# Weight words called for earlier, and the first feed-forward block in the third step, in a fused mLSTM and multiplicative FFN kernel

## The chip, the cores and the metric

The kernel runs on one core of a Trainium2 chip. The metric is device time of one execution in microseconds (us); the figure for the kernel before is the median of seven runs. A profile shows one execution: TensorE (PE, with weight loads as PEld), VectorE (DVE), ScalarE (ACT), GpSimd (POOL), and the queue of SyncE (SP), which issues most of the DMAs.

## The reference, cut to what matters

```python
batch, n_heads, seq, head_dim = (4, 8, 768, 40)      # q, k, v, gates
n_tokens, d_model, d_ff = (3072, 320, 1024)          # w1, w2, w3, w_out (float64 arrays)
for t in range(S):                                   # mLSTM cell
    m_new = max(f[t] + m, i[t])
    C = exp(f[t] + m - m_new) * C + exp(i[t] - m_new) * outer(v[t], k[t])
    n = exp(f[t] + m - m_new) * n + exp(i[t] - m_new) * k[t]
    y[t] = sigmoid(o[t]) * (C @ q[t]) / max(abs(n . q[t]), 1)
x = y as rows of (batch, seq), columns (head, dim)   # 3072 x 320
out = (((x @ w1) * (x @ w2)) @ w3) @ w_out
```

## The kernel before, in words

**The cell** is computed in chunks. A unit n = (c, b) is 128 tokens (the chunk pair c) of one batch b, all 8 heads; there are 24 units, numbered with the batch running fastest. The main loop (L733) makes steps s = 0 to 31. In step s, `quarter_work` (L328) computes on PE the scores `ss` and the new state terms `pc` of unit s, and, for unit s-1, the products `ph` (weights times v) and `pi` (state times q); DVE then makes the output y of unit s-1 (`outputs`, L397: `h`, `den`, y). PE works on quarters of 64 rows and 64 columns, four side by side. For the first `N_DIAG` units (5) `ph` is instead made with heads on the diagonal quarters only, in a bank of its own, and one DVE addition of 328 columns (L405) takes the place of four of 164 (L408).

**What a unit needs.** k and q of the unit are turned (`turn`, L301: eight PE transposes into `pt`, two ACT copies to `kT` and `qT`; from unit 10 by DVE). Its weights `pw` are exp of a row vector of U, spread over 128 partitions, plus a bias (`weights`, L288: eight ACT instructions), masked by POOL (`masks`). U's rows come in one of three ways: by `spread` (L263), sixteen PE matmuls into `ub`, for units 0 to 3; by `rows_of_u` (L283), a DVE transpose of `UT`, for units 4 to 9; and by a DMA from a copy in DRAM, `U_d`, from unit 10. `cols_of_u` (L273) makes `UT` on PE (`pu`) and ACT, at the end of step 1. `weighted` (L317, POOL) scales v.

**The feed-forward part.** `up` and `up_rest` (L588, L601) make one block: for 256 tokens (half of a group of four units) and 256 of the 1024 columns, a = x w1 and b = x w2, each as 8 matmuls of 128 by 256 for the first 256 rows of w and then a rest on quarters for the last 64 rows (`wr`), followed by an ACT copy of a and a DVE product `ab`. x comes from y by `x_trans` (L456): POOL doubles 64 columns (`twice`, L453), three PE transposes `px`, one ACT copy `xT`. 24 blocks are made so, `n_up` (L722) to a step: one in steps 4 and 5, two in steps 6 to 16. Group 0's blocks run over columns 0 to 511 of both halves first. Later groups go by another scheme (`up_by_seven`), which the change leaves alone. w3 and w_out are multiplied into `w3o` in the steps 10 to 17 (`fold`, L244, PE `wp`), and `ffn_out` makes the result.

**Weights come as float64.** `fetch` (L202) has SP load a piece as pairs of 32-bit words (512 KB for w1 and w2) into one of four `raw` buffers, or, first, into `idle` memory (two places in w3o). `scale` (L178) scales the two words, the high one on ACT and the low one on ACT or, with `early`, on DVE; `to_f32` (L188) joins them with two DVE instructions. w1 and w2 are ten pieces in two halves of the columns: for each half four of 128 rows and `wr`. After them come eight of w_out (`wo`) and sixteen of w3. `n_cvt` gives the pieces converted at the end of a step, `n_fetch` the pieces called for by then.

**What sets the order.** PE's instructions are issued in the order of the program (`in_order`, L84), those of ACT, DVE, POOL and SP as well (`keep_order`, L524). So an instruction that waits holds up all behind it on its engine: on SP, a load that waits for a free buffer holds up the loads after it. Four PSUM banks (`mps`, L77) are handed out in turn to `pt`, `px`, `ub`, `ph`, `pa`, `pb` and `wp`. In step s SP calls for unit s+2 (L737).

Of the kernel before, what the change touches and what calls it, by code (L numbers as in the profile page):

```python
# [16 lines left out]
def kernel(  # L17
# [83 lines left out]

    NB, NBQ, NBV = 4, 3, 5
    N_DVE = N_U = 10
    N_DIAG = 5
    q_all = const.tile([P, NBQ * H * DP], FP, name="q_all")
    qbuf = [q_all[:, i * H * DP:(i + 1) * H * DP].rearrange("p (h d) -> p h d", d=DP) for i in range(NBQ)]
    kbuf = [const.tile([P, H, DP], FP, name=f"kbuf{i}") for i in range(NB)]
# [4 lines left out]
    gT = const.tile([P, NT2, BH], FP, name="gT")  # L112
    wT = const.tile([P, NT2, BH], FP, name="wT")
    decay = const.tile([P, B * NP, NT], FP, name="decay")
    UT = const.tile([P, 2, 2, BH], FP, name="UT")
    U_d = dram.tile([NT, BH, L], FP, name="U_d")
    NY = 15
    KC = KF + 1
# [152 lines left out]
        return ub  # L271

    def cols_of_u():  # L273
        pu = mps([P, 2, 2, BH], "pu")
        for x in range(2):
            for e in range(2):
                for t in range(2):
                    for i in range(2):
                        t0 = (1 - i) * P + x * L + t * 32
                        mm(pu[x * L + e * 32:x * L + (e + 1) * 32, t, i], U[:, t0:t0 + 32], ident[0:RG, i * BH:(i + 1) * BH])  # L280
        nc.scalar.copy(out=UT, in_=pu)

    def rows_of_u(n):  # L283
        c, b = divmod(n, B)
        nc.vector.transpose(out=weights_tile(n).rearrange("p h (t i) -> p h t i", t=2),
                            in_=UT[:, :, c - 1, b * H:(b + 1) * H].rearrange("p t h -> p h t").unsqueeze(3).to_broadcast([P, H, 2, 32]))

    def weights(n):  # L288
        c, b = divmod(n, B)
        src = weights_tile(n) if c else spread(n)  # L290
        pw = weights_tile(n)
        for h in range(H):
            nc.scalar.activation(out=pw[:, h, :], in_=src[:, h, :], func=AF.Exp, bias=aT[:, c, b * H + h:b * H + h + 1])  # L293
# [31 lines left out]
        nc.gpsimd.tensor_tensor(out=new, in0=old, op=OP.mult, in1=decay[:, b * NP:(b + 1) * NP, 2 * c + x:2 * c + x + 1]  # L325
                                .to_broadcast([P, NP, D1]))

    def quarter_work(s, rest):  # L328


        rest()

        def part(j, c0, n):
            return cell[j][:, :, c0:c0 + NP * n].rearrange("p x (n d) -> p x n d", d=n)

        ss, pc, pi = part(0, 0, L), part(0, NP * L, D1), part(1, 0, D1)
        ph = [cell[1][:, x, NP * D1:2 * NP * D1].rearrange("p (h d) -> p h d", d=D1) for x in range(2)]
        n = s - 1
        if 0 <= n < NU:
            pw, vt, qT = u_t.pop(n), vbuf[n % NBV], qT_t.pop(n)  # L340
            before = before_t.pop(n)

            if n < N_DIAG:
                ph = mps([P, H, D1], "ph")
                for hq in range(H):
                    for r in halves:
                        mm(ph[r, hq, :], pw[r, hq, :], vt[r, hq, :])
            for hd in range(H // 2 if n >= N_DIAG else 0):
                for x, e in quarters:
                    hq = hd if x == e else hd + H // 2  # L350
                    mm(ph[x][halves[e], hd, :], pw[halves[x], hq, :], vt[halves[x], hq, :])
            for p in range(NP):
                for hip, x in quarters:
                    mm(pi[halves[x], hip, p, :], qT[heads[hip], p, halves[x]], before[x][heads[hip], p, :])
        n, first_read = s, None
        if n < NU:
            c, b = divmod(n, B)
            kt, vw = kbuf[n % NB], vw_t.pop(n)
            ends = range(2 if c < NT2 - 1 else 1)
            first, second, after = state[b]  # L360
            before_t[n] = first, second
            state[b] = after, second, first
            kT, qT, pw = kT_t.pop(n), qT_t[n], u_t[n]
            for p in range(NP):
                for hip, x in quarters:
                    mm(ss[halves[x], hip, p, :], kT[heads[hip], p, halves[x]], qT[heads[hip], p, halves[x]])
            for p in range(NP):
                for x, e in quarters:
                    if x in ends:
                        mm(pc[halves[e], x, p, :], kt[halves[x], 2 * p + e, :], vw[halves[x], 2 * p + e, :])  # L370
        den = None
        if 0 <= s - 1 < NU:
            den = outputs(s - 1, pi, ph)
            den()
        if n < NU:
            pv = pw.rearrange("p (n two) t -> p two n t", two=2)
            first_read = nc.vector.tensor_tensor(out=pv, in0=ss, in1=pv, op=OP.mult)
        with tc.issue_after(first_read.ins) if first_read else nullcontext():
            if den:
                den()  # L380
            if n < NU:

                if c:
                    nc.vector.tensor_tensor(out=second, in0=pc[:, 0], in1=second, op=OP.add)  # L384
                else:
                    nc.vector.tensor_copy(out=second, in_=pc[:, 0])
                if len(ends) > 1:
                    decayed(after, second, n, 1)
            if den:
                den()  # L390
            if n < NU and len(ends) > 1:
                nc.vector.tensor_tensor(out=after, in0=pc[:, 1], in1=after, op=OP.add)
            if den:
                done = den()
        return done if den else first_read
# [89 lines left out]
        nc.sync.dma_start(out=f_sb[r], in_=f_gate.rearrange("b h s -> (b h) s")[:, cs])  # L485
        nc.scalar.dma_start(out=a[r], in_=i_gate.rearrange("b h s -> (b h) s")[:, cs])

    w3o_words = w3o.rearrange("p f d -> p (f d)").bitcast(U32).rearrange("p (n two) -> p n two", two=2)
    load(0, slice(0, 2))
    fetch("w12", 0, 0)  # L490
    load(0, slice(2, 3))
    fetch("w12", 1, 0)
    load(1, slice(0, 2))
    load_o(0)
    load(1, slice(2, 3))
    load_o(1)
    fetch("w12", 2, 0)
    idle += [w3o_words[:, i * CW:(i + 1) * CW] for i in range(2)]

    nc.vector.memset(on, 1.0)  # L500
    nc.vector.memset(on.rearrange("p (c t) -> p c t", t=L)[:, :, 0:1], 0.0)
# [73 lines left out]
    pd = mps([P, B * NP * NT], "pd")  # L575
    for x in range(2):
        mm(pd[halves[x]], odd[:, x].to_broadcast([RG, L]), pick.rearrange("p j g c -> p (j g c)"))
    nc.scalar.copy(out=decay.rearrange("p j c -> p (j c)"), in_=pd)
    nc.scalar.activation(out=g, in_=U, func=AF.Exp)
    scale_next(True)  # L580
    convert()
# [121 lines left out]
    def ffn_out(blocks, pos=None):  # L703
# [5 lines left out]
        for (gr, j), po in zip(blocks, pos):  # L709
# [3 lines left out]
            nc.scalar.dma_start(out=out[t0:t0 + P, :], in_=o_sb)  # L713


    ups = [(0, [f, f + 1], slice(j * 2 * P, (j + 1) * 2 * P)) for part in range(0, FO, FO // 2) for j in range(2)
           for f in range(part, part + FO // 2, 2)]
    ups += [(gr, [f, f + 1], slice(j * 2 * P, (j + 1) * 2 * P)) for gr in range(1, 3) for j in range(2)
            for f in range(0, FO, 2)]
    downs = [(gr, j) for gr in range(NG) for j in range(GT)]  # L720
    sevens = [(gr, f) for gr in range(3, NG) for f in range(FH)]
    n_up = [0] * 4 + [1] * 2 + [2] * 11 + [0] * 15  # L722
    n_seven = [0] * 19 + [1] * 12 + [0]
    n_down = [0] * 17 + [2] * 6 + [1] * 7 + [0, 5]
    w12 = [("w12", i, part) for part in range(2) for i in range(2 * KF + 1)]
    todo = w12[3:] + [("wo", i, 0) for i in range(FO)] + [("w3", ko, part) for ko in range(FO) for part in range(2)]
    n_cvt = [0, 1, 1, 1, 2, 2, 3, 4, 4] + [2] * 7
    n_fetch = [4, 5, 7, 9, 11, 13, 16, 20]
    pinned, ahead = 32, 9
    behind = ExitStack()  # L730
    turned, converted, fetched = 0, 2, 3

    for s in range(len(n_up)):  # L733
        if N_U <= s + 3 < NU:
            load_u(s + 3)
        if s + 2 < NU:
            load(s + 2)  # L737
            load_o(s + 2)
        if s < NU:
# [1 line left out]
                decayed(state[s % B][1], state[s % B][0], s, 0)  # L741
        if NY <= s - 2 < NU:
            send(s - 2)
        elif 0 <= s - 2 < NY:
            twice(s - 2)
        if NY <= s - 2 < NU:
            get_back(s - 2)
# [16 lines left out]
        if seven and s > NU:  # L764
            seven[0]()
        now = [ups.pop(0) for _ in range(n_up[s])]
        open_ups = [up(*x) for x in now]
        def rest():
            for x in open_ups:
                up_rest(*x)  # L770
            if seven:
                seven[2]()

        gated = None
        if s <= NU:
            gated = quarter_work(s, rest)
        else:
            rest()
        with tc.issue_after(gated.ins) if gated else nullcontext():
            if seven:  # L780
                seven[3]()
            if NY <= s - 2 < NU:
                x_turn(s - 2)
            for n in (B, B + 1) if s == 2 else (s + 3,):
                if 2 <= s and n < N_U:
                    rows_of_u(n)
            if N_DVE <= s + 1 < NU:
                gated = turn(s + 1)
# [2 lines left out]
            if s - 2 in range(4 * GT - 1, NU, GT):  # L791
                token_sums((s - 2) // GT)
        if s == 0:
            gate_cols(g, gT, nc.scalar.copy)
        if s == NU:
            cell_psum.close()
            banks.extend([ps_m] * 3 + [ctx.enter_context(tc.tile_pool(name="ps_x", bufs=4, space=bass.MemoryType.PSUM))] * 4)
        if s + 1 < N_DVE:
            turn(s + 1)
            while turned < min(s - 1, NY):  # L800
                x_trans(turned)
                turned += 1
        if s < NU:
            if s + 1 < NU:
                weighted(s + 1)
                weights(s + 1)
                masks(s + 1)
            out_gate(s)
        if s == 1:
            cols_of_u()  # L810
        if s == 0:
            for i, r in enumerate(third):
                nc.sync.dma_start(out=U_d[i * GC:(i + 1) * GC].rearrange("c r t -> r c t"), in_=U3[r])
        with tc.issue_after(gated.ins) if N_DVE <= s + 1 < NU else nullcontext():
            for _ in range(n_cvt[s] if s < len(n_cvt) else 0):
                convert()
                converted += 1
        if s >= ahead:
# [40 lines left out]
```

## Time and profile before

| what | value |
|---|---|
| median of 7 runs | 443.18 us (440.09 to 447.0) |
| time of the profiled execution | 444.08 us |
| its span, first to last instruction | 442.4 us |
| PE busy | 424.6 us, 96% |
| DVE, ACT, POOL busy | 305.4, 150.7, 82.5 us |
| moved by DMA | 51.14 MB, mean 116 GB/s |
| PE waiting for `xT` (ACT L464), for k's DMA, for `wr` (DVE L191) | 4.0, 5.7, 1.2 us |

Busy time is the time in which an engine has an instruction under way. A matmul's duration overlaps its neighbours', so the spacing of groups, as the chain of waits shows it, says more of PE's pace than the mean of one. In a row of the timeline the columns are start and duration of a run of like instructions, engine, line, operation, what is written and read, shape, count, and in brackets how long the engine had been idle before and what released it.

### The profile page before, as it was taken

What the parts mean: (1) busy time and instruction counts of PE and PEld (TensorE: products, weight loads), DVE (VectorE), ACT (ScalarE), POOL (GpSimd) and SP (SyncE); (2) the same over time, 40 slices, a digit from 0 to 9 for tenths busy, and PEclk for the clock granted to TensorE, in tenths of its full rate; (3) what the DMA queues carried; (4) which work ended last, traced back from release to release, by engine and by line L of the source; (5) the groups of instructions that cost most, each with busy time, mean ns of one, the idle gap of its engine ahead of it and who ended that gap; (6) DMA issues with size and microseconds to landing.
All of it is one profiled execution on the core that took longest, in us unless ns stands there. A gap on an engine that the chain in (4) does not pass through costs nothing.

```text
span 442.4 us, 12852 instructions
## 1 busy us (share of the span) xinstructions
PE 424.6 (96%) x5303; PEld 338.0 (76%) x5303; DVE 305.4 (69%) x629; ACT 150.7 (34%) x409; POOL 82.5 (19%) x155
## 2 busy tenths in 40 slices
PE   4997989999799999999999999999999999999996
PEld 3886878877678787887867877868778777777774
DVE  6358668769777797797758769759689776444800
ACT  4557656756454255233303320313210111101110
POOL 3425333321230331133022204202000000000000
PEclk9999999999899999999999999999999999999999
DMA  8999695787997667778456376454121110000001
GB/s 186 172 186 198 142 178 89 168 208 197 191 199 184 167 132 173 184 147 145 96 107 142 88 144 141 116 103 99 46 51 29 39 39 16 15 16 16 1 30 45
DMA packets 135211, 51.14 MB, mean 116 GB/s; under 512 B 109360, under 2 KB 126960, under 8 KB 135152
## 3 DMA queue, kind: packets, MB, share of 16 engines
q1 hardware_dynamic: 131552, 46.29, 51.1%
q10 hardware_dynamic: 3600, 4.03, 2.6%
q8 instruction: 41, 0.67, 0.7%
q14 instruction: 18, 0.15, 0.1%
HBM read 44.50 MB, written 5.80 MB: 114 GB/s over the span
## 4 chain that ended last, share of the span: by engine, by line
PE 91%; DMA 3%; issue 2%; DVE 1%; ACT 1%; SPq 1%; POOL 0%; ACTq 0%; DVEq 0%
PE cell L92 24%; PE pa L92 22%; PE po L92 14%; PE pb L92 14%; PE wp L92 7%; PE p L92 5%; PE pt L95 3%; DMA kbuf<-in_k_dram 2%; PE ub L92 1%; PE px L95 1%; PE ph L92 1%; DMA raw<-in_moe_w_dram 1%; ACT pw L293 0%; DVE h L408 0%; DVE ab L609 0%
## 5 line engine op out<-in xcount | busy, mean ns | idle before, releaser
L92 PE MATMUL pa<-xT,w 128*128 128x256 f32 x240 | 61.6, 388 | 4.0 <-ACT xT L464 4.0
L92 PE MATMUL po<-w3o,ab 128*128 128x320 f32 x224 | 61.8, 433 | 0.0
L92 PEld LDWEIGHTS po<-w3o,ab 128*128 128x128 f32 x224 | 42.5, 190 | 17.2 <-issue 0.4
L92 PEld LDWEIGHTS pa<-xT,w 128*128 128x128 f32 x240 | 45.1, 192 | 12.1 <-ACT xT L464 4.9
L325 POOL TENSOR_TENSOR state<-state,decay 128x164 f32<-128x164 f32 x40 | 19.7, 492 | 174.3 <-DVE state L384 151.1
L298 POOL TENSOR_SCALAR_AFFINE_SELECT pw<-pw 64x512 f32<-64x512 f32 x48 | 37.2, 775 | 56.7 <-ACT pw L293 55.1
L92 PE MATMUL pb<-xT,w 128*128 128x256 f32 x192 | 46.1, 384 | 0.0
L92 PE MATMUL cell<-w3o,ab 128*128 128x320 f32 x160 | 44.0, 432 | 0.0
L293 ACT ACTIVATE pw<-pw,aT 128x64 f32<-128x64 f32 x160 | 40.3, 339 | 2.8 <-ACT o_sb L711 2.8
L92 PEld LDWEIGHTS pb<-xT,w 128*128 128x128 f32 x192 | 37.1, 194 | 5.3
L92 PEld LDWEIGHTS cell<-w3o,ab 128*128 128x128 f32 x160 | 30.5, 190 | 12.0
L92 PE MATMUL pa<-xT,wr 64*64 64x256 f32 x384 | 36.8, 386 | 1.2 <-DVE wr L191 1.2
L656 DVE SCALAR_TENSOR_TENSOR a_sb<-pa,wo 128x512 f32<-128x512 f32 x12 | 8.3, 692 | 41.6 <-PE pa L92 41.6
L608 ACT ACTIVATE a_sb<-pa 128x512 f32<-128x512 f32 x24 | 14.3, 596 | 66.1 <-PE pb L92 66.1
L92 PE MATMUL pb<-xT,wr 64*64 64x256 f32 x384 | 36.2, 380 | 0.0
L92 PE MATMUL wp<-wo,w3T 128*128 128x320 f32 x128 | 35.9, 433 | 0.0
L609 DVE TENSOR_TENSOR ab<-pb,a_sb 128x512 f32<-128x512 f32 x24 | 16.4, 689 | 27.8 <-ACT a_sb L608 27.8
L92 PEld LDWEIGHTS pa<-xT,wr 64*64 64x64 f32 x384 | 19.0, 132 | 16.1 <-issue 8.3
L92 PEld LDWEIGHTS wp<-wo,w3T 128*128 128x128 f32 x128 | 23.7, 190 | 8.9
L711 ACT COPY o_sb<-po 128x320 f32<-128x320 f32 x14 | 6.0, 425 | 67.4 <-PE po L92 67.4
L408 DVE TENSOR_TENSOR h<-cell,h 64x164 f32<-64x164 f32 x76 | 24.7, 326 | 1.4
L92 PEld LDWEIGHTS pb<-xT,wr 64*64 64x64 f32 x384 | 20.2, 133 | 3.0
(135 smaller groups left out, 738.3 us busy)
## 6 DMA issues: line engine op xcount, KB each, us to landing
raw<-in_moe_w_dram SPq DMA_DIRECT2D x64, 128.0 KB, 3.2
kbuf<-in_k_dram SPq DMA_DIRECT2D x24, 160.0 KB, 4.7
vbuf<-in_v_dram SPq DMA_DIRECT2D x24, 160.0 KB, 4.9
o_in<-in_o_gate_dram SPq DMA_DIRECT2D x24, 160.0 KB, 4.6
out_dram<-o_sb ACTq DMA_DIRECT2D x24, 160.0 KB, 1.8
raw<-in_moe_w_dram SPq DMA_DIRECT2D x7, 512.0 KB, 4.9
pw<-U_d SPq DMA_DIRECT2D x28, 128.0 KB, 3.3
raw<-in_moe_w_out_dram SPq DMA_DIRECT2D x8, 320.0 KB, 3.5
```

The costliest lines, as they stand in the source:

```text
L92: in_order(nc.tensor.matmul(out, lhsT=lhsT, rhs=rhs, start=start, stop=stop))
L95: in_order(nc.tensor.transpose(out, in_, ident[0:n, 0:n]))
L293: nc.scalar.activation(out=pw[:, h, :], in_=src[:, h, :], func=AF.Exp, bias=aT[:, c, b * H + h:b * H + h + 1])
L298: nc.gpsimd.affine_select(out=pw[r], in_=pw[r], compare_op=OP.is_ge, fill=0.0, base=0, pattern=[[0, H], [1, L]], channel_multiplier=-1)
L325: nc.gpsimd.tensor_tensor(out=new, in0=old, op=OP.mult, in1=decay[:, b * NP:(b + 1) * NP, 2 * c + x:2 * c + x + 1] .to_broadcast([P, NP, D1]))
L408: nc.vector.tensor_tensor(out=part, in0=ph[x][halves[e]], in1=part, op=OP.add)
L608: nc.scalar.mul(out=a_sb, in_=pa, mul=UP ** -2)
L609: nc.vector.tensor_tensor(out=ab_t[gr][j][:, fs[0]:fs[-1] + 1, t0:t0 + a_sb.shape[-1]], in0=pb, in1=a_sb, op=OP.mult)
L656: nc.vector.scalar_tensor_tensor(out=out, in0=p, scalar=UP ** -2, in1=q, op0=OP.mult, op1=OP.add)
L711: nc.scalar.copy(out=o_sb, in_=po)
```

## The change

- **Words.** Before the loop, five pieces of w1 and w2 are called for in place of three (the whole first half of the columns); the output gate of unit 0 goes behind the third piece and that of unit 1 behind the fourth, and two places in `wo` are added to the idle memory. In step 2 SP is given the other five, three ahead of the k and q of unit 4 and two ahead of its v. Conversions are moved accordingly (`n_cvt`, `between`, `rest`).
- **Blocks.** Group 0's blocks take all 1024 columns of its first 256 tokens first. `n_up` becomes one in steps 2 to 5, two in 6 to 14, one in 15 and 16. The block of step 2 is made in the middle of `quarter_work`, by `between`, after the outputs of unit 1 are complete and before the scores of unit 2. `turn(2)` and `turn(3)` move to steps 2 and 3.
- **U's rows.** `cols_of_u` moves ahead of the loop and gets a third chunk; `rows_of_u` also serves units 1 to 3. The write of `U_d` moves from step 0 to step 4.
- **Units 2 to 4** make `ph` on quarters (`N_DIAG` is 2).

```diff
-    N_DIAG = 5
+    N_DIAG = 2
...
     def weights(n):
         c, b = divmod(n, B)
-        src = weights_tile(n) if c else spread(n)
+        src = weights_tile(n) if n else spread(n)
...
+        den = None
+        if 0 <= s - 1 < NU:
+            den = outputs(s - 1, pi, ph)
+            den()
+            if between:
+                for _ in range(3):
+                    den()
+                den = None
+                between()
         n, first_read = s, None
...
     load(0, slice(0, 2))
     fetch("w12", 0, 0)
     load(0, slice(2, 3))
     fetch("w12", 1, 0)
-    load(1, slice(0, 2))
+    load(1)
+    fetch("w12", 2, 0)
     load_o(0)
-    load(1, slice(2, 3))
+    idle += [words[:, i * CW:(i + 1) * CW] for words in (w3o_words, wo_words) for i in range(2)]
+    fetch("w12", 3, 0)
     load_o(1)
-    fetch("w12", 2, 0)
-    idle += [w3o_words[:, i * CW:(i + 1) * CW] for i in range(2)]
+    fetch("w12", 4, 0)
...
+    cols_of_u()
     nc.scalar.copy(out=decay.rearrange("p j c -> p (j c)"), in_=pd)
+    rows_of_u(1)
...
-    n_up = [0] * 4 + [1] * 2 + [2] * 11 + [0] * 15
+    n_up = [0] * 2 + [1] * 4 + [2] * 9 + [1] * 2 + [0] * 15
...
-    n_cvt = [0, 1, 1, 1, 2, 2, 3, 4, 4] + [2] * 7
-    n_fetch = [4, 5, 7, 9, 11, 13, 16, 20]
+    n_cvt = [1, 0, 3, 0, 1, 2, 2, 3, 2] + [2] * 7
+    n_fetch = [5, 5, 10]
...
-        if s + 2 < NU:
+        if s < 3:
+            if s == 2:
+                for _ in range(3):
+                    fetch(*todo.pop(0))
+            load(s + 2, slice(0, 2))
+            if s == 1:
+                load_o(2)
+            if s == 2:
+                for _ in range(2):
+                    fetch(*todo.pop(0))
+                fetched = 10
+            load(s + 2, slice(2, 3))
+            if s:
+                load_o(s + 2)
+        elif s + 2 < NU:
...
+        if s == 3:
+            turn(3)
         def rest():
             for x in open_ups:
                 up_rest(*x)
             if seven:
                 seven[2]()
+            if s == 3:
+                for _ in range(2):
+                    convert()
+
+        def between():
+            twice(1)
+            weighted(2)
+            for n in range(2):
+                x_trans(n)
+            for _ in range(2):
+                scale_next(True)
+                convert()
+            turn(2)
+            for x in now:
+                up_rest(*up(*x))
...
-            for n in (B, B + 1) if s == 2 else (s + 3,):
-                if 2 <= s and n < N_U:
+            for n in (s + 2,) if s < B else (s + 2, s + 3) if s == B else (s + 3,):
+                if n < N_U:
                     rows_of_u(n)
```

More of the change, by code (lines that the diff above doesn't have):

```diff
@@ L114 @@
     decay = const.tile([P, B * NP, NT], FP, name="decay")
-    UT = const.tile([P, 2, 2, BH], FP, name="UT")
+    UT = const.tile([P, 2, 3, BH], FP, name="UT")
     U_d = dram.tile([NT, BH, L], FP, name="U_d")
@@ L273, in cols_of_u @@
     def cols_of_u():
-        pu = mps([P, 2, 2, BH], "pu")
+        pu = mps([P, 2, 3, BH], "pu")
         for x in range(2):
@@ L277, in cols_of_u @@
                 for t in range(2):
-                    for i in range(2):
-                        t0 = (1 - i) * P + x * L + t * 32
-                        mm(pu[x * L + e * 32:x * L + (e + 1) * 32, t, i], U[:, t0:t0 + 32], ident[0:RG, i * BH:(i + 1) * BH])
+                    for c, of in ((0, slice(0, 2)), (1, slice(2, 3))):
+                        t0 = c * P + x * L + t * 32
+                        mm(pu[x * L + e * 32:x * L + (e + 1) * 32, t, of].rearrange("p c r -> p (c r)"),
+                           U[:, t0:t0 + 32], ident[0:RG, 0:(of.stop - of.start) * BH])
         nc.scalar.copy(out=UT, in_=pu)
@@ L285, in rows_of_u @@
         nc.vector.transpose(out=weights_tile(n).rearrange("p h (t i) -> p h t i", t=2),
[L286 removed]
+                            in_=UT[:, :, (0, 2, 1)[c], b * H:(b + 1) * H].rearrange("p t h -> p h t").unsqueeze(3).to_broadcast([P, H, 2, 32]))
     def weights(n):
         c, b = divmod(n, B)
[L290 removed]
+        src = weights_tile(n) if n else spread(n)
         pw = weights_tile(n)
@@ L326, in decayed, with quarter_work @@
                                 .to_broadcast([P, NP, D1]))
-    def quarter_work(s, rest):
+    def quarter_work(s, rest, between):
         rest()
@@ L370, in quarter_work @@
                         mm(pc[halves[e], x, p, :], kt[halves[x], 2 * p + e, :], vw[halves[x], 2 * p + e, :])
[L371 to L374, printed above, removed]
         if n < NU:
@@ L486 @@
         nc.scalar.dma_start(out=a[r], in_=i_gate.rearrange("b h s -> (b h) s")[:, cs])
-    w3o_words = w3o.rearrange("p f d -> p (f d)").bitcast(U32).rearrange("p (n two) -> p n two", two=2)
+    w3o_words, wo_words = (t.rearrange("p f d -> p (f d)").bitcast(U32).rearrange("p (n two) -> p n two", two=2)
+                           for t in (w3o, wo))
     load(0, slice(0, 2))
@@ L713, in ffn_out @@
             nc.scalar.dma_start(out=out[t0:t0 + P, :], in_=o_sb)
[L716 to L719, printed above, removed]
+    ups = [(gr, [f, f + 1], slice(j * 2 * P, (j + 1) * 2 * P)) for gr in range(3) for j in range(2)
+           for f in range(0, FO, 2)]
     downs = [(gr, j) for gr in range(NG) for j in range(GT)]
     sevens = [(gr, f) for gr in range(3, NG) for f in range(FH)]
-    n_up = [0] * 4 + [1] * 2 + [2] * 11 + [0] * 15
+    n_up = [0] * 2 + [1] * 4 + [2] * 9 + [1] * 2 + [0] * 15
     n_seven = [0] * 19 + [1] * 12 + [0]
@@ L725 @@
     w12 = [("w12", i, part) for part in range(2) for i in range(2 * KF + 1)]
-    todo = w12[3:] + [("wo", i, 0) for i in range(FO)] + [("w3", ko, part) for ko in range(FO) for part in range(2)]
-    n_cvt = [0, 1, 1, 1, 2, 2, 3, 4, 4] + [2] * 7
-    n_fetch = [4, 5, 7, 9, 11, 13, 16, 20]
+    todo = w12[5:] + [("wo", i, 0) for i in range(FO)] + [("w3", ko, part) for ko in range(FO) for part in range(2)]
+    n_cvt = [1, 0, 3, 0, 1, 2, 2, 3, 2] + [2] * 7
+    n_fetch = [5, 5, 10]
     pinned, ahead = 32, 9
     behind = ExitStack()
-    turned, converted, fetched = 0, 2, 3
+    turned, converted, fetched = 0, 2, 5
     for s in range(len(n_up)):
@@ L743 @@
             send(s - 2)
-        elif 0 <= s - 2 < NY:
+        elif 0 <= s - 2 < NY and s != 3:
             twice(s - 2)
@@ L766 @@
         now = [ups.pop(0) for _ in range(n_up[s])]
-        open_ups = [up(*x) for x in now]
+        open_ups = [up(*x) for x in now] if s != 2 else []
+        if s == 3:
+            turn(3)
         def rest():
@@ L772, in rest @@
                 seven[2]()
+            if s == 3:
[12 more added lines that the diff above has]
+                up_rest(*up(*x))
         gated = None
         if s <= NU:
-            gated = quarter_work(s, rest)
+            gated = quarter_work(s, rest, between if s == 2 else None)
         else:
@@ L793 @@
         if s == 0:
+            weighted(1)
+            weights(1)
+            masks(1)
             gate_cols(g, gT, nc.scalar.copy)
@@ L797 @@
             banks.extend([ps_m] * 3 + [ctx.enter_context(tc.tile_pool(name="ps_x", bufs=4, space=bass.MemoryType.PSUM))] * 4)
+        if s in (2, 3):
+            turned, converted = 2, converted + 2
         if s + 1 < N_DVE:
-            turn(s + 1)
+            if s not in (1, 2):
+                turn(s + 1)
             while turned < min(s - 1, NY):
@@ L803 @@
         if s < NU:
-            if s + 1 < NU:
-                weighted(s + 1)
+            if 0 < s < NU - 1:
+                if s != 1:
+                    weighted(s + 1)
                 weights(s + 1)
@@ L808 @@
             out_gate(s)
-        if s == 1:
-            cols_of_u()
-        if s == 0:
+        if s == B:
             for i, r in enumerate(third):
@@ L815 @@
             for _ in range(n_cvt[s] if s < len(n_cvt) else 0):
+                if s == 0:
+                    scale_next(True)
                 convert()
```

## The prediction

> **What bounds the kernel.** I read the page first: span, busy shares and the slices of the span.
>
> ```profile
> span 442.4 us, 12852 instructions
> PE 424.6 (96%) x5303; PEld 338.0 (76%) x5303; DVE 305.4 (69%) x629; ACT 150.7 (34%) x409; POOL 82.5 (19%) x155
> PE   4997989999799999999999999999999999999996
> ```
>
> PE is the bound, and from the slices its holes lie in the first quarter. Then busy time by stretches of the span:
>
> ```profile
> 30.00:35.00 5.00, 4.52 (x125) 4.10 (x125) 4.42 (x12) 3.16 (x12) 1.16 (x2) 1.00 1.04 137
> 35.00:40.00 5.00, 3.46 (x74) 3.08 (x75) 4.51 (x11) 4.04 (x12) 1.88 (x4) 1.00 1.03 274
> 40.00:45.00 5.00, 3.78 (x35) 2.86 (x35) 3.49 (x6) 2.36 (x7) 3.81 (x6) 1.00 0.96 149
> 100.00:120.00 20.00, 17.69 (x217) 13.96 (x216) 17.62 (x32) 11.65 (x26) 4.31 (x8) 0.95 0.95 204
> ```
>
> The columns are stretch, length, busy us of PE, PEld, DVE, ACT and POOL (instructions), granted clock, DMA share, GB/s. Early, PE has holes while DVE is nearly full; from 124 to 430 us PE has none. So work taken out of a late step shortens the run one for one, and costs in an early step only what does not fit the holes. The chain of waits gives PE's pace (start, duration, what):
>
> ```profile
> 22.70 1.90 PE pt L95 x8
> 30.82 1.02 PE pt L95 x8
> 186.00 1.85 PE cell L92 x128
> 188.32 4.31 PE wp L92 x16
> 192.63 1.73 PE pa L92 x8
> 194.36 1.73 PE pb L92 x8
> 201.43 1.85 PE cell L92 x128
> ```
>
> The same eight transposes take 1.90 us at 22.7 and 1.02 at 30.8: PE ran at half pace at first. The last lines are a late step, 186.00 to 201.43, 15.43 us: cell 1.85, `px` 0.48, `wp` 4.31, two blocks of 3.46, and their rests from 199.54 to 201.43, 1.89. **One block is 3.46 + 0.95 = 4.4 us.** Last, the timeline around the hole at 115:
>
> ```profile
> 103.73 8.10 SPq L175 DMA_DIRECT2D raw<-in_moe_w_dram  x15
> ...
> 115.37 0.67 ACT L182 ACTIVATE raw<-raw 128x512 f32<-128x512 f32 x1 [1.06 <-DMA raw<-in_moe_w_dram]
> ...
> 116.49 0.46 ACT L464 COPY xT<-px 128x384 f32<-128x384 f32 x1
> ...
> 117.00 2.99 PE L92 MATMUL pa<-xT,w 128*128 128x256 f32 x8 [2.31 <-ACT xT L464]
> ```
>
> ACT waits for words of w3; behind them stands the `xT` copy, and for it PE waits.
>
> **Term 1, the two blocks moved: -8.8 us.** Steps 15 and 16 lose one block each, 2 x 4.4. They shrink to 11.0 us of PE, while DVE is busy 12.2 in each (the windows of 15.4 us there). DVE then lags by some 2.5 us, but step 17 has 15.4 us of PE for 9.5 of DVE, and step 16's scores need only `kT` and `qT`, made ahead of DVE's conversions; so I cost the lag at nothing. Without that cover it is 1.2 us a step, 2.4.
>
> **Term 2, what the early steps take: +6.0 us.** Before, the cell of step 6 ends at 69.2, with four blocks made; after, six. I laid the new order out by hand with the rows' durations.
> Ahead of step 0, `pu` (PE, 32 instructions; 0.90 at 26, about 1.6 at half pace, from `ub`'s 1.98 against 1.15) goes between `pd` and the scores, where PE idled 0.5 for `vw`. It holds ACT's order by about 1.7 us: `UT` at 13.4, `decay`, g, words to 15.0. DVE gets a transpose (0.70) and its conversion ahead of the scores of unit 0: 16.9 against 15.5. The `ub` of units 1 to 3 go (1.98, 1.66, 1.15 on PE); the transposes add 0.70 each on DVE. They nearly cancel: the outputs of unit 0 start at 21.0 (21.1 before).
> In step 2 DVE no longer interleaves: y of unit 1 is the sum of DVE's rows from there, 0.50 + 0.50 + 0.17 + 0.69 + 0.16 + 0.32 + 0.19 + 0.33 + 0.76 + 0.49 for step 1 with POOL's 0.46, the transpose 0.70, then 0.50 + 0.50 + 0.52 + 0.76 + 0.49: 28.8 us. Before it was 34.7.
> Then POOL 0.31, `px` 0.95, `xT` 0.5 (30.1). ACT scales two pieces (0.7 each), DVE joins them (1.2 each, with gaps): 32.0 and, for `wr`, 33.6. PE turns unit 2 (to 31.9 at half pace), then the block: 35.3 and rest 36.3 at full pace, 38.4 if the clock rises at 36. I take 36.7.
> Now ACT and DVE set the pace. Scores at 37.7; `a_sb` and `ab` 38.0; weights of unit 3, tanh (39.8); three pieces at 1.35 on ACT (0.67 + 0.67) to 43.8; `kT` and `qT` of unit 3 to 45.0; `a_sb` 45.6; two more pieces to 48.3, joined at 49.5. All five have landed by about 39: up to there SP waits for no buffer, and a piece takes about 1.7 us and a unit's load about 1.0 (the landings up to 21 us). Only behind these joins does DVE make outputs of unit 2: 0.50 + 1.34 + 0.17, weights 0.69: 52.2. Here PE waits most. Step 4's block runs 47.3 to 51.7, its cell ends at 54.2. Unit 5 is turned; the block of step 5 waits for a bank that `ab` frees at 55.9, and ends at 60.4, its cell at 62.3. The rest of step 5's end, with `xT` of unit 3, reaches 64.5; two blocks (8.8) and the cell (1.84) then end at 75.2. That is 6.0 later, with two more blocks behind it.
> In this the four additions of `N_DIAG` are in: 1.34 against 0.50 on DVE, 0.62 against 1.0 on PE, for three units. The U_d write moves past nothing that waits: its first reader is in step 7. Each edit's bounds: DVE and ACT additions between 0 (hidden) and their full rows; `pu` from -0.9 (it leaves step 1) to +1.7.
>
> **Term 3, a new wait in step 8: +1.1 us.** Group 1 starts one step earlier, with tokens of unit 5, whose `px` stands right ahead of it. The rows with that order before (39.01 and 58.32, `pa` released by `xT`) show 1.07 us between weight loads, 0.84 on PE; the bound is 0 to 2.3, the worst row.
>
> **Term 4, the hole at 115: -4.2 us.** PE idles 114.7 to 117.0 (2.3), then `pa` takes 2.99 and `pb` 2.42 for 1.73 each (1.95) at the granted half clock. In the old lists four pieces (16 to 19) are converted in step 8 and four called for behind them, so the fourth lands last, at 115. In the new ones step 8 converts two and calls for two, as the steps from 10 on do, where no hole shows. The bounds are 0 and -4.25; I take the latter, since the steady rows are the same case.
>
> Sum: -8.8 + 6.0 + 1.1 - 4.2 = -5.9. Against the profiled execution's own 444.08 (1.7 outside its span) that is 438.2; the runs' median is 0.9 below that execution, so **437.3 us**.
>
> **A rule against the change.** The clock rows: half pace until about 25.7, though PE was busy in all of 15.5 to 25.7; and back to half after a window with 1.09 us of work (114.5 to 117.9). The Trainium skill, "TensorE: Matmul & The Clock Gate", Part 1, says that the clock is at half by default, rises after some 3.4 us of sustained work and falls after an idle window of that length. By the rule PE, which has little to do from 26 to 29 while y of unit 1 is made, would start the block of step 2 cold and be warm within one window, about 1.7 us lost; by the trace, where rising took over 10 us of small matmuls, all of the block could be cold, 4.
>
> **The rivals.**
> *The clock stays at half through the blocks of steps 2 and 3.* For it: the row of 114.5. Against: the rise at 25.7 came in the stretch with sixteen full-size transposes, and the new step 2 has those and a dense block. The first block then takes up to 4.0 more, some in the second: 437.3 + 4 = 441.3, no change.
> *The hole at 115 stays or moves* because the words of w3 still come last: 437.3 + 4.2 = 441.5, no change.
> *The DMAs fall behind: slower.* The new order puts 2.6 MB of words ahead of and among unit 4. From 28.5, with o of unit 3 landed, until k of unit 6, 5.4 MB pass; PE turns unit 6 at about 62. At 190 GB/s (0 to 10) that takes 28 us and nobody waits. Under 160 PE waits; at 137 (30 to 35, unit loads alone) it takes 39.5, unit 6 comes 5.7 late, q 1.2 later, and the words of w3 then are late too, so the 4.2 stays: 437.3 + 11.1 = 448.4. It makes the run slower by over 0.5% from about 147 GB/s down. Against it: words moved at 274 (35 to 40).
> *Better than laid out:* PE warm from 18.9 on, and ACT's order looser: -1.4 and -1.1: 434.8.
>
> **The numbers.** 0.5% (2.2 us) is about what a measurement of this kernel can tell from no change. Chances: forecast 0.54 (434.5 to 440.5), better 0.07, clock 0.14, hole 0.12, DMA 0.13. So faster 0.61, same 0.26, slower 0.13. The range runs from below the better case, 433, to 444, which takes in both middle rivals with errors of 2.5 and leaves out the DMA case and little else.
>
> **What would show it.** Right: step 2's `pa` starts at 30 to 34; `pa` and `pb` of step 3 follow its cell without a gap; the cell of step 6 ends near 75; no idle of over 1 us and no half clock between 100 and 125; steps 15 and 16 last 11.0. Wrong: `pt` of unit 6 released by a DMA; `pa` groups of 3.4 us at 30 to 45; ACT waiting for raw words at 105 to 117; DVE ending late in step 16 with PE waiting in step 17.

## The result, and the profile after

The changed kernel takes 449.31 us (median of 14 runs, 446.37 to 452.11) against 443.91 (35 runs of the kernel before beside them): a ratio of 1.0132, 95% interval 1.0107 to 1.0157. It is slower; 437.3 was forecast, and 449.3 lies above the range.

The page of the kernel after: span, busy times, and two rows of the slices (11.2 us each).

```profile
span 446.8 us, 12660 instructions
PE 422.4 (95%) x5207; PEld 334.2 (75%) x5207; DVE 310.4 (69%) x644; ACT 148.9 (33%) x406; POOL 82.1 (18%) x155
PE   4769999999899999998997999999999999999997
PEclk9959999999999999999998699999999999999999
```

PE has less work (422.4 us for 424.6) in a longer span. New are the 7 in the slice that begins at 235 us, the 8 at 201, and a granted clock of 0.8 and 0.6 in the slices at 235 and 246; in the kernel before, PE had no such slice from 122 us to its last. Next, the chain of waits of the kernel after, at the cells of steps 6, 10, 14, 15 and 16:

```profile
72.64 1.84 PE cell L92 x128
...
126.54 1.84 PE cell L92 x128
...
188.91 1.84 PE cell L92 x128
...
200.02 1.84 PE cell L92 x128
...
212.81 1.84 PE cell L92 x128
```

The cells of steps 6, 10 and 16 in the kernel before (those of 14 and 15 start at 186.00 and 201.43):

```profile
67.38 1.84 PE cell L92 x128
...
124.30 1.84 PE cell L92 x128
...
216.85 1.84 PE cell L92 x128
```

Against these the kernel after is 5.3 late, 2.2 late, 2.9 late, then 1.4 and 4.0 ahead. So to 213 us the plan works, nearly as laid out. At the end of the span it is 4.4 behind: 8.4 us are lost after step 16. The windows of the kernel after say where (length, then busy us of PE, PEld, DVE, ACT, POOL, clock, DMA share, GB/s):

```profile
100.00:120.00 20.00, 18.82 (x231) 15.28 (x230) 17.61 (x37) 14.62 (x37) 7.34 (x12) 1.00 0.90 177
230.00:250.00 20.00, 15.88 (x175) 11.62 (x170) 13.16 (x33) 4.66 (x17) 3.27 (x5) 0.81 0.64 135
```

In the first, PE gained 1.1 us and the clock is whole: the hole at 115 is gone. In the second, PE is idle for 4 of 20 us. The timeline of the kernel after there:

```profile
224.24 0.38 ACTq L723 DMA_DIRECT2D out_dram<-o_sb  x1
226.13 1.09 SPq L150 DMA_DIRECT2D pw<-U_d  x2
228.55 0.38 ACTq L723 DMA_DIRECT2D out_dram<-o_sb  x1
...
229.88 3.87 SPq L440 DMA_DIRECT2D y_d<-y  x2
...
235.69 3.54 SPq L449 DMA_DIRECT2D yb<-y_d  x4
...
240.74 0.58 DVE L456 STREAM_TRANSPOSE xT<-yb 128x384 f32<-128x384 f32 x1 [6.08 <-DMA yb<-y_d]
...
243.25 1.13 PE L92 MATMUL cell<-qT,kT 40*64 40x64 f32 x32 [3.30 <-DVE qT L308]
```

And the same kinds of instruction in the kernel before, with the scores of unit 18 last:

```profile
217.47 1.09 SPq L150 DMA_DIRECT2D pw<-U_d  x2
...
223.58 1.27 SPq L434 DMA_DIRECT2D y_d<-y  x2
...
238.62 0.56 DVE L450 STREAM_TRANSPOSE xT<-yb 128x384 f32<-128x384 f32 x1
...
243.80 0.68 PE L92 MATMUL cell<-qT,kT 40*64 40x64 f32 x32
```

Read from the bottom up. PE waits 3.30 us for `qT` of unit 18. DVE makes it late because the transpose ahead of it (`x_turn`, y of unit 15 come back from DRAM) stood idle 6.08 us for `yb`. `yb` is late because SP sent y 6.3 us later than before (229.88 for 223.58), and because the trip itself, from the first `y_d` to the last `yb`, took 9.4 us for 5.1. SP was late because the load ahead of it, U's rows for unit 20, went out at 226.13; before, it went out at 217.47, 0.6 behind the start of the cell of step 16 (216.85). In the kernel after that cell starts at 212.81, SP has issued the loads ahead by 216.50, and from there it stands still for 9.6 us. The view of waits of SP's queue (in total, times, longest) names whom it waited for:

```profile
SPq L150 <- DMA out_dram<-o_sb: 19.2, 2, 9.7
```

The wait for unit 20 is one of the two, 9.5 us; the longest, 9.7, belongs to a later load of the same line, issued at 266.71. Both waited for an out row of ffn_out, which ACT issues, and which has nothing to do with U. The link is in the compiled program. Each DMA of SP and ACT signals its end on one of eight semaphores, handed out in turn, and a DMA waits until the one that used its semaphore eight places earlier has landed. The program after, in SP's order, its DMAs counted from 0 (the first out row of step 17 took number 6 between 242 and 243):

```
242 L139 gates<-in_k_dram      [waits DMAHW5]
243 L139 gates<-in_k_dram      [waits DMAHW7]
...
248 L139 gates<-in_q_dram      [waits DMAHW5]
249 L150 pw<-U_d (unit 20)     [waits PE,DMAHW6,Activation,Pool]
```

In the kernel before, no out row stood between those loads of step 16, and the load of unit 20 followed another of SP's own. With shorter steps 15 and 16 the out rows of step 17 slipped in among them.

### The profile page after: what moved, and what is told of

Its sections match the earlier page's. It is cut to its first block, busy times and chain, and to the rows that moved or that the text cites. A ratio compares the mean times of both kernels' runs of the same rounds, so it can differ in the third digit from the quotient of the medians.

```text
span 446.8 us, 12660 instructions
## 1 busy us (share of the span) xinstructions
PE 422.4 (95%) x5207; PEld 334.2 (75%) x5207; DVE 310.4 (69%) x644; ACT 148.9 (33%) x406; POOL 82.1 (18%) x155
## 4 chain that ended last, share of the span: by engine, by line
PE 79%; DVE 6%; DMA 4%; ACT 4%; SPq 4%; issue 2%; POOL 1%; POOLq 0%; DVEq 0%
PE cell L92 20%; PE pa L92 20%; PE pb L92 12%; PE po L92 12%; PE wp L92 7%; PE p L92 5%; SPq L139 1%; PE px L95 1%; DMA out_dram<-o_sb 1%; PE pt L95 1%; DMA q_all<-in_q_dram 1%; DMA y_d<-y 1%; ACT pw L294 1%; POOL state L326 1%; DMA raw<-in_moe_w_dram 1%
## 5 line engine op out<-in xcount | busy, mean ns | idle before, releaser
L92 PE MATMUL pa<-xT,w 128*128 128x256 f32 x240 | 63.3, 396 | 2.8 <-ACT xT L470 2.8
L92 PEld LDWEIGHTS pa<-xT,w 128*128 128x128 f32 x240 | 46.1, 198 | 11.2 <-ACT xT L470 3.8
L294 ACT ACTIVATE pw<-pw,aT 128x64 f32<-128x64 f32 x184 | 46.4, 339 | 2.8 <-ACT o_sb L721 2.3
L299 POOL TENSOR_SCALAR_AFFINE_SELECT pw<-pw 64x512 f32<-64x512 f32 x48 | 38.5, 801 | 43.9 <-ACT pw L294 42.4
L414 DVE TENSOR_TENSOR h<-cell,h 64x164 f32<-64x164 f32 x88 | 28.7, 326 | 1.6
```

What stands on the lines that cost most here:

```text
L92: in_order(nc.tensor.matmul(out, lhsT=lhsT, rhs=rhs, start=start, stop=stop))
L299: nc.gpsimd.affine_select(out=pw[r], in_=pw[r], compare_op=OP.is_ge, fill=0.0, base=0, pattern=[[0, H], [1, L]], channel_multiplier=-1)
L414: nc.vector.tensor_tensor(out=part, in0=ph[x][halves[e]], in1=part, op=OP.add)
```

## The experiments

The compared kernel before had a median of 444.2 us beside the first four runs, 444.05 beside the second four and 444.69 beside the last three. "After" is 449.31. Two theories at the start: **the queue** (SP held by an out row, hence `qT` late, the hole, and then the clock) and **the short steps** (steps 15 and 16 leave DVE with more work than PE, and DVE ends late). Beside these, which part of the 8.4 is the hole and which the clock.

### The out rows off the shared semaphores

```diff
-            nc.scalar.dma_start(out=out[t0:t0 + P, :], in_=o_sb)
+            (nc.gpsimd if (gr, j) in ((0, 0), (0, 1)) else nc.scalar).dma_start(out=out[t0:t0 + P, :], in_=o_sb)
```

> The changed kernel with one edit: the first two results (step 17) are written to DRAM by POOL's queue, not by ACT's. Theory (held queue): in the changed kernel SP's load of U's rows for unit 20 stands idle until the first result has landed, at 226.1, some 9.7 us; the two share one of eight completion semaphores, which SP's and ACT's DMAs use in turn. Behind it on SP the trip of unit 15's y through DRAM is late, so DVE turns k and q of unit 18 late, PE waits 3.3 us near 240 and its clock falls to half for 10.2 us. With the results off that turn, the load goes out by 217, PE has no hole near 240 and no half clock from 242 to 252, and the kernel keeps the 4 us that it led by in step 17: 440 to 441. Rival (DVE short): the shorter steps 15 and 16 leave DVE's work of those steps to step 17 and 18; the hole and the half clock stay, 448 to 450. Rival (trip too long): the load goes out early but the trip of y does not fit the shorter steps even so: a hole of 1 to 3 us stays, 442 to 448.

Measured: 442.85 (440.66 to 444.89), 0.997 of before, interval 0.994 to 1.0008, 6.5 under the kernel after. Work, steps and DVE's load are unchanged; only who issues two rows. The timeline of this run:

```profile
203.04 0.54 PE L95 MATMUL px<-ident,y 128*128 128x128 f32 x2 [1.74 <-issue]
...
214.57 1.09 SPq L150 DMA_DIRECT2D pw<-U_d  x2
```

The load goes out at 214.57, 0.6 behind the start of its cell (213.95), and there is neither a hole nor half clock near 240 (PE busy 20.00 of 20 us from 230 to 250, clock 1.00). The queue theory holds. That it isn't 440 to 441, and no clear gain on the kernel before, has two causes in the profile. One is the first row: inside the three transposes of step 16 PE stood 1.74 us, for nothing that the profile shows, and after this the clock was at half from 203 to 206.4. The other is the same fault one step on. SP waits for another out row, 11.4 us, among the loads of k:

```profile
225.79 13.06 SPq L139 DMA_DIRECT2D q_all<-in_k_dram  x4
...
SPq L139 <- DMA out_dram<-o_sb: 14.1, 2, 11.4
```

(The second line is from the view of waits.) Behind it y of unit 16 goes out at 247.60, DVE stands idle 7.41 us for it, and the scores of units 19 and 20 are 20.14 us apart (18.63 in the kernel before), with PE waiting for DVE: 1.5 us. No run was made without this second wait.

### Without y's trip through DRAM

```diff
-    NY = 15
+    NY = 18
```

with x of units 15 to 17 made by transposes on PE, where `x_turn` stood.

> The changed kernel with x of units 15 to 17 made by PE transposes (three of 128 by 128 and an ACT copy for each, in steps 17 to 19) in place of y's trip through DRAM. SP's load for unit 20 still waits for the first result. Held queue: the load still goes out at about 226, but DVE no longer waits for the trip ahead of k and q of unit 18, so the hole near 240 and the half clock go; PE has 3 times 0.5 us more: 441 to 443. DVE short: the hole stays, since DVE is relieved of only 0.6 us a step: 447 to 449.

Measured: 441.69 (439.77 to 443.8), ratio 0.996, interval 0.9926 to 0.9993. The load of unit 20 is as late as in the kernel after (224.71), and nobody minds: the scores of unit 18 start at 238.63. So the late load costs through y's trip, which stands behind it on SP; nothing else is seen to wait for it.

### Work for PE in the hole

```diff
+            if s == 18:
+                fill = mps([P, 512], "fill")
+                for _ in range(6):
+                    mm(fill, ident, w1[:, 0, 0:512])
```

ahead of the scores of unit 18.

> The kernel after, with six matmuls of 128 by 512 added, whose result nobody reads, ahead of the scores of unit 18 in step 18, where PE stood idle from 239.95 to 243.25. They change nothing on SP, so the load of unit 20 still waits for the out rows. Theory (most of the loss at 240 is the clock, which falls to half after the hole and stays there for 10.2 us; the hole alone is 3.3): PE keeps the full clock, the time is about 449.3 - 4.4 = 445. Rival (the clock is not what costs; the wait for y of unit 15 is paid in full by whatever stands behind it): 448 to 450. The matmuls themselves take about 6 x 0.43 = 2.6 us, inside the hole.

Measured: 446.61 (445.57 to 447.82), 1.005 of before, interval 1.0022 to 1.0078. It misses 445 because I sized the filler wrongly: each of the six is two instructions, twelve of 0.43, and they end 2 us behind `qT` (244.3). The timeline of this run:

```profile
241.05 5.42 PE L92 MATMUL fill<-w,ident 128*128 128x512 f32 x12
246.40 0.69 PE L92 MATMUL cell<-qT,kT 40*64 40x64 f32 x32
```

The scores of unit 18 start at 246.40, 3.15 us later than in the kernel after, and yet the run ends earlier: from that start to the end of the span it is 445.2 - 246.40 = 198.8 us, against 446.8 - 243.25 = 203.55. In the kernel before it is 442.4 - 243.80 = 198.6. The difference, 4.75 us, is what the kernel after loses behind its hole; the windows of this run show full clock from 238 to 260. Up to 0.82 of it is a wait of PE for DVE's `w3T` at 247.17, which comes from the late trip too and which the run with the fillers doesn't have. So **the clock's price is 3.9 to 4.75 us**, and the rival, by which it cost nothing, falls. The 8.4 are 3.3 of hole, 3.9 to 4.75 of half clock, and the rest waiting for DVE and small change.

### Short steps elsewhere

```diff
-    n_up = [0] * 2 + [1] * 4 + [2] * 9 + [1] * 2 + [0] * 15
+    n_up = [0] * 2 + [1] * 4 + [2] * 7 + [1] * 2 + [2] * 2 + [0] * 15
```

> The kernel after, with the two short steps moved from 15 and 16 to 13 and 14; the number of blocks is the same. Instructions of the end of step 16 are then as in the kernel before, and the load of unit 20 follows another load on its semaphore in place of an out row. Theory (SP's queue, held by that out row, cost the 8.4 us): the load is issued right behind the cell of step 16, no hole near 240, 449.3 - 8.4 - 1.5 = 439 to 441, and less if the idle 1.46 of step 16 goes too. Rival (DVE, which the short steps leave with more work than PE, is what runs late): DVE stands out in steps 14 and 15 in place of 16 and 17, with PE waiting for it, and the time is 444 to 449.

Measured: 438.77 (438.33 to 439.89), ratio 0.9891, interval 0.986 to 0.9922. As the queue theory had it. Steps 13 and 14 last 11.11 us each on PE (cells from 157.5, 168.7 and 179.8), and the idle time in step 16's transposes is gone too. The rival has a small share: DVE runs late, PE waits for it once, and step 15 lasts 16.6 us for 15.4.

```profile
183.06 4.55 PE L92 MATMUL wp<-wo,w3T 128*128 128x320 f32 x16 [0.80 <-DVE w3T L239]
```

The waits of SP's queue in this run, for the same line:

```profile
SPq L150 <- PE cell L92: 0.4, 1, 0.4
```

The out rows have left the list of this line. **The change itself is worth 5.3 us** with the short steps put two steps earlier.

### Short steps early, none late

```diff
-    n_up = [0] * 2 + [1] * 4 + [2] * 9 + [1] * 2 + [0] * 15
+    n_up = [0] * 2 + [1] * 6 + [2] * 9 + [0] * 15
```

> The changed kernel with one edit: one block in steps 2 to 7 and two in 8 to 16, so that steps 15 and 16 are as before and steps 6 and 7 are the short ones. Held queue and DVE short alike: no hole near 240 and no half clock there; steps 6 and 7 are bound by DVE rather than PE, at 9 to 10 us for 7.6 of PE, so that 2 to 4 of the 8.8 us are lost: 441 to 444. Rival (the early part carries its cost into the late steps, through buffers or queues): the hole near 240 stays, 447 to 450.

Measured: 436.71 (435.81 to 437.95), ratio 0.9855, interval 0.9804 to 0.9907. That is 4.3 us below the range that I expected: I had taken steps 6 and 7 for bound by DVE, which would have kept the time of the blocks taken out there. The cell of step 6 starts at 67.29, 5.35 earlier than in the kernel after for one block less (4.4), and that of step 10 at 117.41, 9.1 earlier for two (8.8). Nothing was hidden there. (Five profiles of kernels with the same steps up to there, the kernel after among them, have that cell of step 6 between 71.51 and 72.64: differences of up to 1.1 us in the early steps are no more than this spread.)

### The lists of words alone

The kernel before, with the word lists only:

```diff
-    n_cvt = [0, 1, 1, 1, 2, 2, 3, 4, 4] + [2] * 7
-    n_fetch = [4, 5, 7, 9, 11, 13, 16, 20]
+    n_cvt = [0, 1, 1, 1, 2, 3, 4, 4, 2] + [2] * 7
+    n_fetch = [4, 5, 7, 9, 11, 14, 18, 22]
```

> The kernel before with only its lists of conversions and calls changed: steps 5 to 8 convert 3, 4, 4, 2 pieces where they converted 2, 3, 4, 4, and the calls stand at 14, 18, 22 after steps 5 to 7 where they stood at 13, 16, 20. Theory (the hole near 115 is ACT waiting for the last of four pieces called for together): PE's idle and the half clock between 105 and 122 go, 4.2 us: 439 to 441. Rival (the hole has another cause, such as the trip of the words behind unit loads): the hole stays, 443 to 445.

Measured: 440.02 (438.94 to 442.01), ratio 0.9912, interval 0.9883 to 0.994. The cell of step 10 starts at 120.39, 3.9 before that of the kernel before, 0.35 of it from ahead of step 6. Term 4 stands by itself, with no other part of the change.

### Where step 2 stands

Three variants of the 436.71 kernel ask what sets its early pace. First, five units on the diagonal again (`N_DIAG = 5`):

> The variant with one block in steps 2 to 7 and two in steps 8 to 16 (436.7), with the diagonal-only products of units 2 to 4 put back as in the kernel before: DVE's additions shrink from 1.34 to 0.50 us in three units, PE's products take about 0.4 more in each. If DVE sets the pace of steps 3 to 5, the time falls by up to 3 x 0.84 - 3 x 0.4 = 1.3, to 435.4; if PE or ACT does, it rises by up to 1.2, to 437.9.

Measured: 438.85 (437.22 to 440.48), ratio 0.9891, interval 0.9862 to 0.9919. Nothing shows DVE setting the pace of steps 3 to 5: the cell of step 6 starts at 68.13 for 67.29, 0.8 later, where a pace set by DVE would have made it up to 1.3 earlier. By step 13 the two are level (163.43 for 163.69); the other 1.5 us is a single idle time on PE in step 14 (1.55 at 180.6), again with no cause in the profile, so this run only puts the edit's cost between -0.3 and +0.8.

Second and third, filler between the two turns of x in step 2, ten and five:

```diff
-            for n in range(2):
-                x_trans(n)
+            x_trans(0)
+            fill = mps([P, 512], "fill")
+            for _ in range(5):
+                mm(fill[:, 0:P], ident, ident)
+            x_trans(1)
```

> The same variant (436.7), with ten matmuls of 128 by 128 whose result nobody reads between the two turns of x in step 2, to keep PE busy while y of unit 1 is made. If the clock's half pace at the block of step 2 costs what its rows show (2.22 us for a group of 8 in place of 1.73), warming PE gives 1 to 1.7: 435 to 435.7. If PE is not what step 2 waits for, no change: 436.5 to 437.

> The same variant (436.7), with five matmuls of 128 by 128 (ten instructions of 0.22 us, 2.2 in all) whose result nobody reads, where PE idles 2.44 us in step 2 for y of unit 1; ten of them took 4.47 and came out 2.0 us later than y. If half pace in step 2 is on the path: turns and block there run 1.6 us shorter, 435.1 to 436. If DVE and ACT set steps 3 to 5 anyway: no change, 436.5 to 437.

Measured: with ten 437.09 (436.62 to 440.19), ratio 0.9862, interval 0.9829 to 0.9895; with five **435.78** (434.89 to 436.25), ratio 0.9815, interval 0.9783 to 0.9847, the fastest of all. Timeline of the kernel after, then of the one with five:

```profile
30.90 3.54 PE L92 MATMUL pa<-xT,w 128*128 128x256 f32 x8
```

```profile
26.26 2.34 PE L92 MATMUL fill<-ident 128*128 128x128 f32 x10
28.90 0.87 PE L95 MATMUL px<-ident,y 128*128 128x128 f32 x3 [0.30 <-DVE y L429]
...
30.57 1.89 PE L92 MATMUL pa<-xT,w 128*128 128x256 f32 x8
```

With five, `pa` runs at full pace (1.89 for 3.54), and the scores of step 2 start at 35.03; 35.94 without filler, 37.02 in the kernel after. The granted clock doesn't tell them apart: from 23 to 34 it is 1.00 here and 0.55 in the kernel after, but it is 1.00 as well in the run with short steps at 13 and 14, which has no filler, and `px` takes 0.87 or 0.88 in all three, where the run with ten fillers shows 0.53. So the pace is read from the rows. From the start of this `px` to the scores it is 6.1 us here and 5.9 in the run with both edits (below), and 7.1 to 8.5 in the eight profiles of kernels with this step 2 and no filler. The lead of 0.9 is still there in step 5 (58.30 for 59.23; 58.78 at the earliest without filler), and the medians differ by as much, 0.93. The intervals of the two kernels overlap, so on times alone the gain is likely, not certain. Ten were too many: y was ready at 28.6, and the filler ended at 30.6.

### The wait left in step 10

In the 436.71 kernel PE still waits 2.3 us at 109.5 for an `xT` copy that stands behind words on ACT.

```diff
-    n_cvt = [1, 0, 3, 0, 1, 2, 2, 3, 2] + [2] * 7
+    n_cvt = [1, 0, 3, 0, 1, 2, 2, 3, 1] + [2] * 3 + [3] + [2] * 3
```

> The variant with one block in steps 2 to 7 and two in steps 8 to 16 (436.7), with one piece converted in step 8 in place of two and three in step 12. In that variant PE waits 2.3 us for an xT copy at 109.5, with ACT ahead of it waiting for words called for at 102.6. With one piece fewer freed and called for, only one of the two pieces that ACT scales there is late. Theory (the words called for last set that wait): the wait shrinks to 0.6 or less, 436.7 - 1.7 = 435. Rival (the wait is taken over by another load or conversion, or moves to step 12): 436.5 to 438.

> Both of these edits. If they act apart and both theories hold: 436.7 - 1.7 - 1.2 = 433.8; if neither holds, 436.5 to 438.

Measured: 439.86 (438.97 to 441.68), ratio 0.9907, interval 0.9876 to 0.9938; with the filler 436.65 (436.03 to 437.62), ratio 0.9838, interval 0.9806 to 0.9871. A miss: the wait is taken over, as the rival had it, but the first time lies 1.9 above the rival's range too. The timeline of the first:

```profile
108.85 2.88 PE L92 MATMUL pb<-xT,w 128*128 128x256 f32 x8 [2.40 <-ACT xT L470]
...
133.14 0.55 PE L95 MATMUL px<-ident,y 128*128 128x128 f32 x3 [1.51 <-ACT pw L294]
```

With one piece of w3 fewer, PE has one `wp` less (4.31 us) ahead of that wait. The copy comes earlier, but PE more so; the hole stays, the clock falls after it (0.84 from 110 to 120), and a second hole comes at 131.6. Here a lighter load on the late engine did nothing, since the bound engine got lighter by more.

## Why the prediction was wrong

**What bounds the kernel: the step that failed.** "Work taken out of a late step shortens the run one for one" was read from PE's busy share and one chain, of the kernel before. It holds only while every chain that PE doesn't set keeps ahead of PE, and I gave no number for how far ahead y's trip through DRAM was. The rows of before have it: `x_turn` at 238.62 and the scores of unit 18 at 243.80, 5.2 apart, where the kernel after, with PE waiting, shows 2.5 from the one to the other (240.74 to 243.25). So there were 2.7 us to spare. With `x_turn` 2.1 later and PE 4.0 earlier, 6.1 were needed: 3.4 are missing, the hole.

**Term 1 (-8.8).** Step 15 shrank by 4.3 as said (15.43 to 11.11) and step 16 by 2.6 (15.42 to 12.79), with 1.46 us of unexplained idle in its transposes. Then 8.4 were given back: at the scores of unit 18 the kernel after is 0.55 ahead of the kernel before, so 3.45 of its 4.0 are gone, nearly all in the hole, and behind it 4.95 more go (203.55 for 198.6), most of it to the clock. The term is worth -6.9 at its place and +1.5 at the end. "I cost the lag at nothing" was about DVE and was right for these two steps: DVE is idle 4.72 us ahead of 229.20 in the kernel after, before the outputs. With the short steps at 13 and 14 the lag did cost, 1.2 us in step 15. What would have told was SP's view of waits, which already in the kernel before has a load waiting for an out row:

```profile
SPq L139 <- DMA out_dram<-o_sb: 8.6, 3, 4.3
```

I didn't ask what that row would do to the queue when steps shift. The warning that I named, "DVE ending late in step 16 with PE waiting in step 17", pointed at the right symptom with the wrong engine and one step too early.

**Term 2 (+6.0).** The cell of step 6 ends at 74.48 for 75.2 forecast and 69.22 before: +5.3 (the other four profiles with these early steps: +4.1 to +5.2). Step 2's `pa` starts at 30.9 (30 to 34 forecast), the scores of step 2 at 37.0 (37.7).

**Terms 3 and 4 (+1.1 and -4.2).** From the end of cell 6 to the end of cell 10 the kernel takes 53.9, 56.9 before: -3.0 for -3.1. Term 4 alone, in its own run, gave -3.6 between these cells and -4.2 in the median. A wait of 1.18 for the same copy is left at 116.3, but the clock stays whole there.

Together terms 2 to 4 say +2.9 at step 14, and 2.9 is what the chain shows; in part by luck, since it is 2.2 at step 10, and another 0.7 that no term has comes by step 14. Where no out row holds the load of unit 20, the forecast of 437.3 is near: short steps at 13 and 14 give 438.77. In the place that the change gave them, with two out rows on POOL's queue, it was 442.85, with the idle time in step 16 and one more wait for an out row still in it.

**The rivals.** The clock in step 2 cost one group at half pace (3.34 for 1.73, 1.6 us), not the whole block. The rule of the Trainium skill, "TensorE: Matmul & The Clock Gate", Part 1, weighed in the prediction, has one window of some 3.4 us either way. In step 2 the row agrees with it: PE is busy from 28.53 on, and the clock is back at 34, time for one whole window. At 242 it fell although no 3.4 us were idle, and came back after the first window that was busy throughout (below). "Half pace until about 25.7" in the kernel before is read from the durations (`pt` 1.90 for 1.02); the granted clock is 1.00 there. DMAs did not fall behind: 185 GB/s from 28.5 to 62, and `pt` of unit 6 waited for none. The slower side that came true, a hole behind a queue with some 4 us of half clock, was none of my rivals; the 0.13 for "slower" stood on another mechanism.

## What to carry to other kernels

Before work is taken out of a step, list each chain that ends in the later steps without being PE's own (here y by way of DRAM and back), by how much it is ahead of PE, and which queues it stands in: what holds it there doesn't come forward along with PE. Read the waits of the queues as well as those of the engines: where a DMA is released by an unrelated one, look in the compiled program whether the two share a semaphore; here they did, and a change of order moved that link. The hole of 3.3 us on PE cost about 4 more through the half clock after it, and useless work put into it took 2.7 us off the time although it ended 2 us too late.

## What was not expected of the hardware

The clock went down after a window of about 3.4 us with 1.15 us of PE work and came back late. The windows of the kernel after:

```profile
238.80:242.20 3.40, 1.15 (x65) 1.02 (x64) 1.46 (x3) 2.80 (x10) 0.00 (x0) 1.00 0.55 140
242.20:245.60 3.40, 2.35 (x65) 2.27 (x66) 3.37 (x7) 0.00 (x0) 0.00 (x0) 0.54 0.67 175
245.60:249.00 3.40, 2.58 (x6) 1.54 (x6) 3.26 (x11) 0.00 (x0) 0.00 (x0) 0.50 0.94 172
249.00:252.40 3.40, 3.40 (x9) 2.70 (x8) 2.90 (x8) 0.00 (x0) 2.21 (x4) 0.50 0.47 76
```

It came back (0.96 from 252.40 to 255.80) only after the window in which PE was busy throughout; 2.35 and 2.58 of 3.40 did not do, so the stay was 10.2 us, three such windows. A hole of 2.3 us at 109.5 left the clock whole in the 436.71 kernel, one of 2.24 at 110.4 lowered it in the kernel with ten fillers. In step 16 holes of 1.74 and 2.14 lowered it (0.54 and 0.52 from 203 to 206.4), and holes of 1.19 and 1.46 did not. What else than the length decides, no run here settles.

Open stays the idle time on PE of 1.2 to 2.1 us that five of the kernels show in late steps (at 201 to 202 in the kernel after and the three runs with its step 16; at 181 with five diagonal units). The kernel after:

```profile
203.59 0.44 PE L95 MATMUL px<-ident,y 128*128 128x128 f32 x2 [1.46 <-issue]
```

It stands at one place in the program for all that share step 16, and the profile names no releaser for it. No run was made for it.
